# Block 1's doubled input in two transfers of 64 partitions from SP, and block 0's taps ahead of the first weights on DVE

## The chip, the core and the metric

The kernel runs on one core of one Trainium2 chip. The metric is the device time of one execution in microseconds. The core's engines are called PE (TensorE, matrix products), PEld (its weight load), DVE (VectorE), ACT (ScalarE), POOL (GpSimd) and SP (SyncE, which here only issues transfers). Each engine works through its own list of instructions in order.

## The reference: what is computed

```python
w = np.exp(weight - max); w = w / (sum(w) + 1e-9)      # 8 heads, 7 taps each
x_unf = x_pad[:, idx, :].reshape(B, S, K, H, group)    # causal windows of 7 tokens
x = np.einsum('hk,bskhg->bshg', w, x_unf)              # x becomes 8192 tokens x 192 channels
h = x @ w_in                                           # 192 -> 2048
g = np.where(h >= 1, h, np.where(h <= -1, 0, (h + 1) ** 2 / 4))
x = g @ w_out                                          # 2048 -> 192
h = x @ w_in2
x = (h * sigmoid(1.702 * h)) @ w_out2
```

A softmax-weighted convolution of seven taps along the tokens is followed by two feed-forward layers with different gates.

## The kernel before, in words

Data lie with the channels on the partitions. The 8192 tokens are 16 blocks of 512. The 192 channels are 128 ("a") and 64 ("b"); `xa[i]` holds the a part of block i with 6 tokens of lead, 128 rows of 518, and `xb` holds the b parts of two blocks in one tile.

Each number is split into a high and a low part (`fp32r`), and a product is made of three matmuls: high by high, low by high, high by low. A matmul takes half of the rows (64) of the array, and two of them run side by side on the two halves. Work on a block and a layer is a phase, (1, 0) being layer 1 of block 0. A phase has 16 units of 128 hidden channels. For two units at a time PE makes the first product into a `pair` tile, ACT and DVE make the gate and split it (`a`, then `ghi` on ACT and `glo` on DVE), and two such steps later PE adds the second product into `acc`. Step k stands for units 2k and 2k+1 of the whole list. The units of the first two phases, which are blocks 0 and 1 of layer 1, are mixed, so that each weight tile serves both while later weights are still being prepared.

The weights come as 64-bit floats. A weight tile (layer n, group g) lands in `raw`, and then ACT scales its high words (`wa`, L148), DVE shifts the low words (`wd`, L151) and joins both (L154), ACT or DVE casts the high part (L160), and DVE subtracts to get the low part (L165, L170). For the first two groups this is done in two pieces, the first of 448 columns. For later groups `convert_at` places these operations by step numbers: the table `steps` gives for each group the step of its fetch, scale, shift, join, high and low. Operations of one step on DVE run before that step's gate. `raw` has three buffers, so a fetch waits until an older tile has been scaled and shifted.

The convolution of the first two blocks is done in a special way, to be ready early:

- Block 0's a part (`ca`, operations `a0`): seven taps on DVE (L190, L191).
- The b part of both blocks (`cb_ps`, operations `b_ops`): PE, with the taps on diagonal matrices (`diag`, L237).
- Block 1's a part (`ca_ps`, operations `a1`): PE takes two taps in one matmul (L226). For that its input is doubled: tile `pair_x[j]` holds channels 64j to 64j+63 twice, on partitions 0 to 63 as they are and on partitions 64 to 127 shifted by one token. ACT first writes the seventh tap into the bank (`tap6`, L245), and the first of PE's three pairs of taps follows.

The program then runs lists of these operations in a written order, and `sc`, `sh`, `jo`, `hi`, `lo` are the five weight operations with the group number and an "o" for the second piece. `a0h`, `a0l`, `b0h`, ... are the splits of the convolution sums (`xah`, `xbh` on ACT at L250, `xal`, `xbl` on DVE at L253). PE's own order is: `b_ops`, the first piece of `a1`, the first products of units 0 and 1 (`straight`, `last`, `crossed`), the rest of `a1`, the first products of units 2 and 3, then the regular steps.

In the kernel before, ACT issues the two loads of `pair_x`, one for each tile of 128 partitions. The source is written with the shift as its outermost dimension, which has two entries:

```python
nc.scalar.dma_start(t, shifted(xa[1, j * H : (j + 1) * H], 0, 1, [PAD + T, H], [1, PAD + T]))
```

SP issues all other loads: `taps`, block 0's `xa`, the first `xb`, then the weights. The semaphores of transfers go round, eight of them, so an issue waits until the transfer eight places before has landed.

Of the kernel before, what the change touches and what calls it, by code (L numbers as in the profile page):

```python
# [8 lines left out]
F32 = mybir.dt.float32  # L9
# [6 lines left out]
P = 128  # L16
T = 512
# [3 lines left out]
def kernel(  # L21
# [21 lines left out]
    nc = tc.nc  # L43
    NBLK, D, _ = out.shape
    K = taps_in.shape[2]
    NF, _, WT = w1.shape
# [3 lines left out]
    PAD = K - 1  # L50
    H = P // 2
# [8 lines left out]
    xt_p = ctx.enter_context(tc.tile_pool(name="xt", bufs=2))  # L60
# [38 lines left out]
        nc.vector.reciprocal(share, share)  # L99
        nc.gpsimd.tensor_mul(taps, exps, share.unsqueeze(2).to_broadcast([P, 2, K]))  # L100

    def shifted(src, first, shift, *rest):
        return bass.AP(tensor=src.tensor, offset=src.offset + first, ap=[[shift, 2], *rest])

    def in_halves(t):
        return t.rearrange("(s p) c -> s p c", s=2)


    words = {1: w1, 2: w2}
# [396 lines left out]
    def finish(p, step):  # L506
        n, i = phases[p]
        if n == 1:
            up, down, add, bh, bl, ah, al = finish_ops(p)
            if i < B:  # L510
                groups = [(up, down, add, ah, al, bh, bl)]
            else:
                groups = [(up, ah, al), (down, add), (bh, bl)]
            for k, ops in enumerate(groups):
                for op in ops:
                    at(step + 2 * k, op) if k else op()
        else:
            acc_a, acc_b = accs.pop(p)
            o = o_p.tile([P, 2, T], F32, tag="o", name="o")
            nc.scalar.copy(o[0:DB, 1], acc_b[DB:P])  # L520

            def rest():
                nc.vector.tensor_add(o[0:DB, 1], acc_b[0:DB], o[0:DB, 1])
                nc.scalar.copy(o[:, 0], acc_a)
                nc.sync.dma_start(out[i, 0:P], o[:, 0])
                nc.sync.dma_start(out[i, P:D], o[0:DB, 1])

            if p < len(phases) - 1:
                at(step + 2, rest)
            else:  # L530
                nc.vector.tensor_add(o[0:DB, 1], acc_b[0:DB], o[0:DB, 1])
                near, far = slice(0, T // 2), slice(T // 2, T)
                nc.scalar.copy(o[:, 0, near], acc_a[:, near])
                nc.sync.dma_start(out[i, 0:P, near], o[:, 0, near])
                nc.scalar.copy(o[:, 0, far], acc_a[:, far])
                nc.scalar.dma_start(out[i, 0:P, far], o[:, 0, far])
                nc.sync.dma_start(out[i, P:D], o[0:DB, 1])
# [10 lines left out]
    plan, xt, raw = {}, {}, {}  # L548
# [26 lines left out]
    def fetch_x(*which):  # L575
        for part, i in which:
            xt[part, i] = x_load(part, i)
# [11 lines left out]
    with tc.manual_schedule():  # L589
        first, second = halves_of  # L590
        nc.sync.dma_start(taps, taps_in)
        fetch_x((0, 0), (1, 0))
        for g in (0, 1):
            fetch_w(1, g, first)
        for g in (0, 1):
            fetch_w(1, g, second)

        cb_ps, ca_ps = [bank(k, f"cb_ps{k}") for k in (3, 1)], bank(2, "ca_ps")
        warm_up(ca_ps, (T, T // 4), True)
        make_identity(nc, ident)  # L600
        less_max(taps)
        nc.scalar.activation(exps, taps, AF.Exp)

        es_ps = bank(0, "es_ps")[:, 0 : 2 * K].rearrange("p (j k) -> p j k", k=K)
        spread_exps(es_ps)
        warm_up(ca_ps, (7 * T // 8,), False)
        table = const.tile([P, 1], F32, name="table")
        for i in range(B):
            x1[i] = new_xs()
        ca = cv_p.tile([P, T], F32, tag="cva", name="cva")  # L610
        a0 = conv_taps(0, xt[0, 0], ca, exps)
        db = o_p.tile([P, K, P], F32, tag="o", name="diag")
        db = [db[:, k] for k in range(K)]
        diagonals(1, db[0:2])
        nc.scalar.copy(exps_s, es_ps)
        diagonals(1, db, 2)
        da = [f32(t).rearrange("p (k c) -> p k c", c=H) for t in new_xs()[0:2]]
        da = [[d[:, m] for m in range(K // 2)] for d in da]
        double_diagonals(da)
        wide = a_p.tile([P, 2, T], F32, tag="a", name="xt1").rearrange("p k t -> p (k t)")  # L620
        pair_x = [xt_p.tile([P, T + 128], F32, tag="xt0", name="xt"), wide]
        pair_x = [t[:, 0 : PAD + T] for t in pair_x]
        for j, t in enumerate(pair_x):
            nc.scalar.dma_start(t, shifted(xa[1, j * H : (j + 1) * H], 0, 1, [PAD + T, H], [1, PAD + T]))  # L624
        b_ops = conv_by_quarters(xt[1, 0], cb_ps, db)
        a1 = conv_by_sides(pair_x, ca_ps, da)
        tap6 = last_tap(pair_x, ca_ps)

        def run(*ops):
            for op in ops:  # L630
                op()

        def parts_of(g):
            s, made = raw.pop((1, g)), weight_tiles()
            return [weight_ops(1, g, s, lambda: made, cols) for cols in halves_of]

        def put_sum(i, part):
            c = (cb_ps[i] if part else ca if i == 0 else ca_ps)
            hi, lo = x1[i][2:] if part else x1[i][:2]
            return [lambda: high_of_sum(part, hi, c), lambda: low_of_sum(part, hi, lo, c)]  # L640

        steps = ((0, 1, 1, 1, 2, 2), (0, 2, 2, 3, 4, 5), (1, 3, 3, 4, 4, 6), (2, 5, 5, 6, 6, 7), (3, 7, 7, 8, 8, 9))
        steps += ((5, 8, 8, 9, 9, 10), (6, 10, 10, 11, 11, 12), (8, 11, 12, 13, 13, 14), (9, 12, 14, 15, 15, 16))
        steps += ((11, 15, 16, 16, 16, 17),)
        for k, when in enumerate(steps, 2):
            convert_at(1 + k // NG, k % NG, *when)
        for g in range(4, NG):
            k = 10 + 2 * g
            convert_at(2, g, k - 3, k - 1, k, k, k, k + 1)
        for j in range(1, NBLK // B):  # L650
            conv_at(j)

        def of(ops, step):
            return ops.get(step, [])

        (sc0, sh0, jo0, hi0, *lo0), (sc0o, sh0o, jo0o, hi0o, *lo0o) = parts_of(0)
        (sc1, sh1, jo1, hi1, *lo1), (sc1o, sh1o, jo1o, hi1o, *lo1o) = parts_of(1)
        (a0h, a0l), (b0h, b0l), (b1h, b1l), (a1h, a1l) = (put_sum(*k) for k in ((0, 0), (0, 1), (1, 1), (1, 0)))
        run(*b_ops)
        run(lambda: nc.scalar.activation(table, ident[:, 0:1], AF.Gelu_apprx_sigmoid))  # L660
        run(*a0[0:5], softmax_taps, sc0, sh0, jo0, hi0, *tap6, *a0[5:], sc1, *lo0, sh1, a0h, a0l, jo1, b0h, b0l)
        straight, crossed, last, closing = first_only(0)
        run(a1[0], straight, last, lambda: crossed(closing), *a1[1:])
        run(hi1, sc0o, sc1o, sh0o, jo0o, *lo1, hi0o, sh1o, b1h, jo1o, *lo0o, b1l)
        early, square, bound, high, low = gate_ops(0)
        run(early, lambda: square(0), lambda: square(1), lambda: bound(0), lambda: bound(1))
        run(*of(fetches, 0), a1h, a1l, lambda: high(0), lambda: high(1), lambda: low(0), lambda: low(1), hi1o, *lo1o)
        straight, crossed, last, closing = first_only(2)
        run(straight, last, lambda: crossed(closing))
        early, square, bound, high, low = gate_ops(2)  # L670
        scale, (shift, join) = of(act, 1), of(dve, 1)
        run(*of(fetches, 1), early, lambda: square(0), lambda: square(1), shift, *scale, lambda: bound(0))
        run(lambda: bound(1), join, *(lambda f=f, k=k: f(k) for f in (high, low) for k in (0, 1)))

        def beside(step):
            for op in plan.get(step, []):
                op()

        def finish_if_last(u, step):
            if 0 <= u < len(units) and units[u][1] == NF - 1 and units[u][0]:  # L680
                finish(units[u][0], step)

        beside(0)
        beside(1)
        for u in range(LAG, len(units) + LAG + 4, 2):
            v, step = u - LAG, u // 2
            if u < len(units):
                both(u, v)
                run(*of(fetches, step), *of(dve, step))
                if v + 1 == unit_at[0, NF - 1]:  # L690
                    gates_beside_finish(u, 0, of(act, step))
                else:
                    gates(u, of(act, step))
            elif v < len(units):
                gemm2(v)
                gemm2(v + 1)
            beside(step)
            finish_if_last(v + 1, u + 1)
# [55 lines left out]
```

## Time and profile before

| | |
|---|---|
| runs | 1141.98, 1142.46, 1144.1 us, median 1142.46 |
| profiled execution | 1141.74 us, span of its instructions 1139.9 us |
| PE | 98% of the span, granted clock 0.993 of full speed on average |
| DVE, ACT | 62% and 73% of the span |

The span runs from the first instruction to the last; 1.84 us lie around it. Busy shares are means over the whole span, so the start of the kernel, which the change touches, has to be read in its own window. Starts of instructions below are in microseconds from the start of the span.

### The profile page before, as it was taken

To read this page: it belongs to the slowest core of one execution; us is meant where nothing else is said; L and a number is where in the kernel's file an instruction comes from. 1 tells how busy PE (TensorE), PEld (TensorE's weight loads), DVE (VectorE), ACT (ScalarE), POOL (GpSimd) and SP (SyncE) were. 2 spreads that over 40 slices of the span, in tenths; PEclk is the share of its full clock that TensorE was granted. 3 is DMA by queue.
4 is the path that set the end of the run, shared out by engine and by line. 5 is a ranking of instruction groups with operands and counts; after the bars stand their busy time and mean duration, and the time that the engine had idled before them with its cause. 6 is when DMAs were issued, how large, how long until landed. Compare 5 with 4: busy or idle time off the path is not lost.

```text
span 1139.9 us, 23934 instructions
## 1 busy us (share of the span) xinstructions
PE 1120.0 (98%) x9790; PEld 1095.8 (96%) x9790; DVE 710.5 (62%) x1098; ACT 831.0 (73%) x1312; POOL 5.3 (0%) x14
## 2 busy tenths in 40 slices
PE   4999999999999999999999999999999999999998
PEld 1788999999999999999999999999999999999998
DVE  3998758684656746566564755647566475665533
ACT  3999768876768777686776767767687776867764
POOL 1000000000000000000000000000000000000000
PEclk7999999999999999999999999999999999999999
DMA  3433101000000001000010000100001000000000
GB/s 120 143 108 112 29 24 52 1 1 10 25 29 15 2 24 29 11 15 10 16 29 11 15 10 15 39 3 14 11 15 38 15 1 10 16 10 15 1 1 28
DMA packets 23872, 30.71 MB, mean 27 GB/s; under 512 B 3284, under 2 KB 15828, under 8 KB 23764
## 3 DMA queue, kind: packets, MB, share of 16 engines
q1 hardware_dynamic: 23360, 28.53, 8.7%
q8 instruction: 77, 1.26, 0.5%
q10 hardware_dynamic: 404, 0.66, 0.2%
q14 instruction: 31, 0.25, 0.1%
HBM read 19.22 MB, written 6.29 MB: 22 GB/s over the span
## 4 chain that ended last, share of the span: by engine, by line
PE 97%; DMA 2%; SPq 0%; DVE 0%; ACT 0%; issue 0%; ACTq 0%; DVEq 0%
PE acc L449 50%; PE pair L449 46%; DMA xt<-in_xa_dram 1%; PE acc L423 0%; PE ca_ps L226 0%; SPq L128 0%; DMA raw<-in_w_dram 0%; ACT ghi L359 0%; ACTq L624 0%; DVE wd L154 0%; SPq L183 0%; DVE wt L165 0%; DVE glo L363 0%; ACT ca_ps L245 0%; DVE a L355 0%
## 5 line engine op out<-in xcount | busy, mean ns | idle before, releaser
L449 PE MATMUL acc<-ghi,wt 64*128 64x512 f32 x3048 | 678.0, 387 | 0.0
L449 PE MATMUL acc<-glo,wt 64*128 64x512 f32 x2032 | 586.4, 386 | 0.0
L449 PEld LDWEIGHTS acc<-ghi,wt 64*128 64x128 f32 x3048 | 488.8, 184 | 3.2
L363 DVE TENSOR_TENSOR glo<-a,ghi 128x512 fp32r<-128x512 f32 x512 | 342.7, 691 | 224.5 <-ACT ghi L359 206.3
L449 PE MATMUL pair<-xah,wt 64*128 64x512 f32 x2048 | 451.6, 388 | 1.2 <-DVE wt L165 1.1
L359 ACT CAST ghi<-a 128x512 fp32r<-128x512 f32 x512 | 314.8, 622 | 44.1 <-DVE a L355 34.9
L449 PEld LDWEIGHTS acc<-glo,wt 64*128 64x128 f32 x2032 | 338.1, 184 | 2.4
L449 PEld LDWEIGHTS pair<-xah,wt 64*128 64x128 f32 x2048 | 302.9, 185 | 7.6 <-ACT xbh L250 1.6
L449 PE MATMUL pair<-xal,wt 64*128 64x512 f32 x1024 | 306.8, 387 | 0.0
L449 PE MATMUL pair<-xbh,wt 64*128 64x512 f32 x1024 | 282.6, 386 | 0.0
L355 DVE SCALAR_TENSOR_TENSOR a<-pair,a 128x512 f32<-128x512 f32 x256 | 164.9, 686 | 164.5 <-PE acc L449 123.1
L348 ACT ACTIVATE a<-pair 128x512 f32<-128x512 f32 x256 | 152.4, 595 | 146.7 <-PE pair L449 146.7
L449 PE MATMUL pair<-xbl,wt 64*128 64x512 f32 x512 | 197.1, 387 | 0.0
L449 PEld LDWEIGHTS pair<-xbh,wt 64*128 64x128 f32 x1024 | 188.3, 185 | 1.3
L346 ACT ACTIVATE a<-pair 128x1024 f32<-128x1024 f32 x128 | 131.6, 1028 | 66.3 <-PE pair L449 64.7
L449 PEld LDWEIGHTS pair<-xal,wt 64*128 64x128 f32 x1024 | 151.9, 185 | 1.3
L351 ACT ACTIVATE a<-a 128x512 f32<-128x512 f32 (+1 forms) x242 | 146.4, 649 | 4.1
L449 PEld LDWEIGHTS pair<-xbl,wt 64*128 64x128 f32 x512 | 94.1, 184 | 0.6
L191 DVE SCALAR_TENSOR_TENSOR cva<-xt,taps,cva 128x512 f32<-128x512 f32 x84 | 63.0, 750 | 1.5
L191 DVE SCALAR_TENSOR_TENSOR cvb<-xt,taps,cvb 128x512 f32<-128x512 f32 x42 | 31.5, 750 | 0.7
L154 DVE SCALAR_TENSOR_TENSOR wd<-wa,wd 128x768 uint32<-128x768 uint32 (+2 forms) x18 | 15.6, 867 | 4.0 <-ACT wa L148 3.4
L226 PE MATMUL ca_ps<-xt,xah 128*64 128x512 f32 x6 | 3.9, 761 | 14.0 <-ACT ca_ps L245 14.0
(68 smaller groups left out, 255.9 us busy)
## 6 DMA issues: line engine op xcount, KB each, us to landing
raw<-in_w_dram SPq DMA_DIRECT2D x48, 128.0 KB, 2.2
xt<-in_xa_dram SPq DMA_DIRECT2D x15, 259.0 KB, 2.8
out_dram<-o SPq DMA_DIRECT2D x15, 256.0 KB, 2.0
raw<-in_w_dram SPq DMA_DIRECT2D x48, 64.0 KB, 2.3
raw<-in_w_dram SPq DMA_DIRECT2D x16, 192.0 KB, 2.6
out_dram<-o SPq DMA_DIRECT2D x17, 128.0 KB, 2.2
xt<-in_xb_dram SPq DMA_DIRECT2D x8, 259.0 KB, 3.1
xbh<-xbh SPq DMA_DIRECT2D x14, 128.0 KB, 2.2
```

Source lines behind the costliest of these rows:

```text
L154: nc.vector.scalar_tensor_tensor(d(), a().bitcast(U32), 3, d(), op0=ALU.logical_shift_left, op1=ALU.bitwise_or)
L191: return lambda: nc.vector.scalar_tensor_tensor(c, x, w, c, op0=ALU.mult, op1=ALU.add)
L226: nc.tensor.matmul(c[side], d[j][m], x, start=False, stop=m == K // 2 - 1)
L346: nc.scalar.activation(a[:, k], h[:, k], AF.Relu, bias=0.5, scale=0.5)
L348: nc.scalar.activation(a[:, k], h[:, k], AF.Gelu_apprx_sigmoid)
L351: nc.scalar.activation(a[:, k], a[:, k], AF.Square)
L355: nc.vector.scalar_tensor_tensor(a[:, k], h[:, k], 1.0, a[:, k], op0=ALU.max, op1=ALU.min)
L359: nc.scalar.copy(halves[u + k][0], a[:, k])
L363: nc.vector.tensor_sub(lo, a[:, k], f32(hi))
L449: mm = nc.tensor.matmul(banks[n], w, r, start=n in fresh, stop=ends.get(n) == k)
```

## The change

SP issues the input of `pair_x`, ahead of the weights, in two transfers. Each goes to 64 partitions and fills both slots (j = 0 and 1), with the rows as the outermost dimension on both sides. ACT issues none of them. The doubled tile moves into the buffer `o` (each of its two rows 32 elements longer), and the diagonals move into a buffer of `a`. The order on ACT and DVE at the start changes, and so do two rows of `steps`.

```diff
-    def shifted(src, first, shift, *rest):
-        return bass.AP(tensor=src.tensor, offset=src.offset + first, ap=[[shift, 2], *rest])
+    def load_twice(t, src):
+
+        _, rows, width = src.shape
+        for s in (0, 1):
+            moved = bass.AP(tensor=src.tensor, offset=src.offset + s, ap=[[width, rows], [rows * width, 2], [1, width]])
+            nc.sync.dma_start(t[s * H : (s + 1) * H], moved)
...
-            o = o_p.tile([P, 2, T], F32, tag="o", name="o")
+            o = o_p.tile([P, 2, T + 32], F32, tag="o", name="o")[:, :, 0:T]
...
         fetch_x((0, 0), (1, 0))
+        pair_x = o_p.tile([P, 2, T + 32], F32, tag="o", name="xt")[:, :, 0 : PAD + T]
+        load_twice(pair_x, xa[1].rearrange("(j p) c -> j p c", j=2))
+        pair_x = [pair_x[:, j] for j in (0, 1)]
...
-        db = o_p.tile([P, K, P], F32, tag="o", name="diag")
-        db = [db[:, k] for k in range(K)]
+        db = a_p.tile([P, 2, T], F32, tag="a", name="diag").rearrange("p k t -> p (k t)")
+        db = [db[:, k * P : (k + 1) * P] for k in range(K)]
...
-        wide = a_p.tile([P, 2, T], F32, tag="a", name="xt1").rearrange("p k t -> p (k t)")
-        pair_x = [xt_p.tile([P, T + 128], F32, tag="xt0", name="xt"), wide]
-        pair_x = [t[:, 0 : PAD + T] for t in pair_x]
-        for j, t in enumerate(pair_x):
-            nc.scalar.dma_start(t, shifted(xa[1, j * H : (j + 1) * H], 0, 1, [PAD + T, H], [1, PAD + T]))
...
-        steps = ((0, 1, 1, 1, 2, 2), (0, 2, 2, 3, 4, 5), (1, 3, 3, 4, 4, 6), (2, 5, 5, 6, 6, 7), (3, 7, 7, 8, 8, 9))
+        steps = ((0, 1, 1, 1, 2, 2), (0, 2, 3, 3, 3, 4), (1, 4, 4, 5, 5, 6), (2, 5, 5, 6, 6, 7), (3, 7, 7, 8, 8, 9))
...
-        run(*a0[0:5], softmax_taps, sc0, sh0, jo0, hi0, *tap6, *a0[5:], sc1, *lo0, sh1, a0h, a0l, jo1, b0h, b0l)
+        run(*a0[0:5], softmax_taps, *tap6, *a0[5:], sc0, sh0, a0h, jo0, hi0, a0l, b0h, *lo0, sc1, sh1, b0l)
...
-        run(hi1, sc0o, sc1o, sh0o, jo0o, *lo1, hi0o, sh1o, b1h, jo1o, *lo0o, b1l)
+        run(sc0o, jo1, hi1, sh0o, jo0o, sc1o, *lo1, hi0o, sh1o, b1h, jo1o, *lo0o, b1l)
```

On ACT, at the start, after the diagonals, the rows of before are these (`wa<-raw 128x448` is `sc0` or `sc1`, `ca_ps<-xt` is `tap6`):

```order
L624 DMA xt<-in_xa_dram 128x1x518
L624 DMA xt_166<-in_xa_dram 128x1x518
L660 ACT_TABLE_LOAD
L660 ACTIVATE table<-ident 128x1
L148 ACTIVATE wa<-raw 128x448
L160 CAST wt_92<-wd 128x448
L245 ACTIVATE ca_ps<-xt,exps_s 64x512
L245 ACTIVATE ca_ps<-xt_166,exps_s 64x512
L148 ACTIVATE wa<-raw 128x448
L250 ACTIVATE xah<-cva,share 128x512
```

And of the change, at the same place:

```order
L659 ACT_TABLE_LOAD
L659 ACTIVATE table<-ident 128x1
L246 ACTIVATE ca_ps<-xt,exps_s 64x512 x2
L149 ACTIVATE wa<-raw 128x448
L251 ACTIVATE xah<-cva,share 128x512
L161 CAST wt_92<-wd 128x448
L251 ACTIVATE xbh<-cb_ps_120,share 128x512
L149 ACTIVATE wa<-raw 128x448
```

The two issues are gone, and `tap6` stands ahead of the first scaling instead of behind the first cast.

On DVE, after the reciprocal of the softmax (`wd<-raw` is `sh`, `wd<-wa,wd` is `jo`, `cva<-xt,exps,cva x2` the last two of block 0's seven taps), the rows of before are these:

```order
L151 TENSOR_SCALAR wd<-raw 128x448
L154 SCALAR_TENSOR_TENSOR wd<-wa,wd 128x448
L191 SCALAR_TENSOR_TENSOR cva<-xt,exps,cva 128x512 x2
L165 TENSOR_TENSOR wt_92<-wd,wt_92 128x384
L151 TENSOR_SCALAR wd<-raw 128x448
L253 SCALAR_TENSOR_TENSOR xal<-cva,share,xah 128x512
```

And of the change:

```order
L192 SCALAR_TENSOR_TENSOR cva<-xt,exps,cva 128x512 x2
L152 TENSOR_SCALAR wd<-raw 128x448
L155 SCALAR_TENSOR_TENSOR wd<-wa,wd 128x448
L254 SCALAR_TENSOR_TENSOR xal<-cva,share,xah 128x512
L166 TENSOR_TENSOR wt_92<-wd,wt_92 128x384
L152 TENSOR_SCALAR wd<-raw 128x448
```

The two taps come first, and the low part of block 0's sum comes ahead of the low part of the first weights.

On DVE in steps 2 to 5, the rows of before, from the low part of group 2 to the low part of group 3, are these (`a<-pair,a` and `glo` belong to the gates):

```order
L165 TENSOR_TENSOR wt_92<-wd,wt_92 128x640
L170 TENSOR_TENSOR wt_92<-wd,wt_92 128x2x64
L151 TENSOR_SCALAR wd<-raw 128x768
L355 SCALAR_TENSOR_TENSOR a<-pair_351,a 128x512 x2
L363 TENSOR_TENSOR glo<-a,ghi 128x512 x2
L154 SCALAR_TENSOR_TENSOR wd<-wa,wd 128x768
L151 TENSOR_SCALAR wd<-raw 128x768
L355 SCALAR_TENSOR_TENSOR a<-pair_420,a 128x512 x2
L363 TENSOR_TENSOR glo<-a,ghi 128x512 x2
...
L363 TENSOR_TENSOR glo<-a,ghi 128x512 x2
L165 TENSOR_TENSOR wt_92<-wd,wt_92 128x640
```

And of the change, over the same stretch:

```order
L166 TENSOR_TENSOR wt_92<-wd,wt_92 128x640
L171 TENSOR_TENSOR wt_92<-wd,wt_92 128x2x64
L356 SCALAR_TENSOR_TENSOR a<-pair_350,a 128x512 x2
L364 TENSOR_TENSOR glo<-a,ghi 128x512 x2
L152 TENSOR_SCALAR wd<-raw 128x768
L155 SCALAR_TENSOR_TENSOR wd<-wa,wd 128x768
L356 SCALAR_TENSOR_TENSOR a<-pair_418,a 128x512 x2
L364 TENSOR_TENSOR glo<-a,ghi 128x512 x2
L166 TENSOR_TENSOR wt_92<-wd,wt_92 128x640
```

The shift of group 3 has moved out of step 2 into step 3, and the low part of group 3 stands one gate earlier, in step 4. Group 4's shift, join and cast follow it a step later than before.

## Rows read from the trace of the kernel before

**Rows 1.** The page, part 1: busy time, share of span, instructions

```profile
PE 1120.0 (98%) x9790; PEld 1095.8 (96%) x9790; DVE 710.5 (62%) x1098; ACT 831.0 (73%) x1312; POOL 5.3 (0%) x14
```

**Rows 2.** Waits by engine, first 45 us: total us, times, longest us

```profile
PE ca_ps L226 <- ACT ca_ps L245: 14.0, 1, 14.0
...
ACT ca_ps L245 <- DMA xt<-in_xa_dram: 11.0, 2, 5.7
```

**Rows 3.** Chain that ended last, first 60 us: start, duration, what

```profile
9.29 15.46 DMA xt<-in_xa_dram
...
25.62 2.06 PE ca_ps L226 x4
27.69 2.25 PE pair L449 x10
29.98 0.96 PE pair L449 x6
30.94 1.87 PE ca_ps L226 x8
32.81 1.60 PE pair L449 x12
```

**Rows 4.** Windows: busy us of each engine, granted clock, DMA share, GB/s

```profile
2.00:8.00 6.00, 5.99 (x37) 2.43 (x40) 4.23 (x10) 2.54 (x10) 3.77 (x6) 1.00 0.76 226
...
6.00:8.00 2.00, 2.00 (x24) 0.64 (x20) 1.90 (x5) 0.00 (x0) 2.00 (x4) 1.00 0.68 186
...
18.00:24.00 6.00, 0.00 (x0) 0.00 (x0) 0.00 (x0) 0.69 (x1) 0.00 (x0) 0.50 0.13 50
...
26.00:28.00 2.00, 2.00 (x6) 0.39 (x5) 1.31 (x3) 1.23 (x3) 0.00 (x0) 0.50 0.00 0
...
60.00:80.00 20.00, 20.00 (x178) 16.55 (x178) 18.99 (x32) 18.57 (x24) 0.00 (x0) 1.00 0.35 100
```

**Rows 5.** Transfers issued in the first 8 us, the plain load: count, KB each, median us to landing

```profile
xt<-in_xa_dram SPq DMA_DIRECT2D x1, 259.0 KB, 2.6
```

**Rows 6.** ACT in order of time: start, duration, instruction, idle before and releaser

```profile
3.94 1.57 ACT L211 ACTIVATE diag<-ident,exps 128x128 f32<-128x128 f32 x5
...
9.85 1.28 ACT L660 ACT_TABLE_LOAD   x1 [4.33 <-DMA xt<-in_xa_dram]
11.14 0.20 ACT L660 ACTIVATE table<-ident 128x1 f32<-128x1 f32 x1
...
12.54 0.56 ACT L160 CAST wt<-wd 128x448 fp32r<-128x448 f32 x1 [0.69 <-DVE wd L154]
18.76 0.69 ACT L245 ACTIVATE ca_ps<-xt,exps_s 64x512 f32<-64x512 f32 x1 [5.66 <-DMA xt<-in_xa_dram]
```

**Rows 7.** DVE: timeline, its busy time in one window, one group of lines

```profile
7.90 0.17 DVE L99 RECIPROCAL share<-share 128x2 f32<-128x2 f32 x1
...
12.42 1.53 DVE L191 SCALAR_TENSOR_TENSOR cva<-xt,exps,cva 128x512 f32<-128x512 f32 x2
...
32.70 1.29 DVE L355 SCALAR_TENSOR_TENSOR a<-pair,a 128x512 f32<-128x512 f32 x2 [0.70 <-ACT a L351]
...
8.09:32.65 24.56, 8.28 (x17) 0.72 0.32 98
...
L154 DVE SCALAR_TENSOR_TENSOR wd<-wa,wd 128x448 uint32<-128x448 uint32 x2 | 1.2, 622 | 3.4 <-ACT wa L148 3.4
```

**Rows 8.** PE in order of time: the last of b_ops, and step 6

```profile
9.73 1.90 PE L237 MATMUL cb_ps<-xt,diag 64*64 64x512 f32 x16
...
54.25 0.50 PE L449 MATMUL pair<-xah,wt 64*128 64x512 f32 x2 [1.08 <-DVE wt L165]
```

**Rows 9.** DVE in steps 2 and 5, and PE where step 4 begins

```profile
42.11 0.56 DVE L151 TENSOR_SCALAR wd<-raw 128x768 uint32<-128x768 uint32 x1
...
44.01 1.29 DVE L363 TENSOR_TENSOR glo<-a,ghi 128x512 fp32r<-128x512 f32 x2
...
44.01 0.73 PE L449 MATMUL pair<-xah,wt 64*128 64x512 f32 x4
```

More of the change, by code (lines that the diff above doesn't have):

```diff
@@ L100, in softmax_taps @@
         nc.gpsimd.tensor_mul(taps, exps, share.unsqueeze(2).to_broadcast([P, 2, K]))
-    def shifted(src, first, shift, *rest):
-        return bass.AP(tensor=src.tensor, offset=src.offset + first, ap=[[shift, 2], *rest])
-    def in_halves(t):
-        return t.rearrange("(s p) c -> s p c", s=2)
+    def load_twice(t, src):
[3 more added lines that the diff above has]
+            nc.sync.dma_start(t[s * H : (s + 1) * H], moved)
     words = {1: w1, 2: w2}
```

## The prediction

> **What bounds the kernel now.** I read the busy shares first: PE is at work for 98% of the span [rows 1], so only time in which PE waits or runs slowly can be won. The waits name the place. Within the first 45 us PE waits once, for 14.0 us, for ACT to write `ca_ps`, and ACT in turn waits 11.0 us, in two pieces, for the two loads of `xt` that it issued itself [rows 2]. The chain of work that ended last goes the same way: 15.46 us of a transfer from 9.29 on, then ACT, then PE's `a1` at 25.62 [rows 3]. PE's part before it, `b_ops`, ended at 9.73 + 1.90 = 11.63 [rows 8].
>
> Two costs follow from that gap. The first is the gap itself. The second is the clock, which the windows show: it stands at 1.00 up to 8 us, at 0.50 (the 1.2 GHz level) in 18 to 24, where PE does nothing, and still at 0.50 in 26 to 28, where PE is busy again [rows 4]. In the chain, four matmuls of `a1` took 2.06 us there, while eight took 1.87 us later; the first products of units 0 and 1 (18 matmuls in two pieces, 27.69 to 30.94) took 3.25 us, while twelve such took 1.60 us at the full clock [rows 3], so 18 take 2.4.
>
> Later PE loses 1.08 us once, in step 6, to the low part of group 3's weights [rows 8]. From 60 us on PE is busy without a break [rows 4], and there nothing can be won.
>
> **The loads.** From 18 to 24 us almost nothing but the doubled loads moves, and the core moves 50 GB/s at a DMA share of 0.13 [rows 4]: 0.13 of 16 engines is two engines, at 25 GB/s each. The ordinary `xa` load, of the same 259 KB, landed in 2.6 us [rows 5].
>
> The rule of the Trainium skill that bears on this is in DMA: Bandwidth & Descriptors, section "Why a DMA increments its semaphore by 16 and not by 1": a transfer uses the largest number of engines up to 16 that divides the slowest dimension of both its sides. By it the old loads (128 and 2) get two engines, with which the trace's 0.13 agrees, and the new ones (64 and 64) get 16. The same page, section "Rules for kernel authors", speaks against halves: two transfers to disjoint halves of the partitions follow one another on the same engines, and one of 128 is advised. By that the two loads would simply come one after the other, as the bytes below are added up.
>
> No row shows a 64 x 2 x 518 transfer. The nearest rows are the plain `xa` load, as the good end, and 50 GB/s on two engines, as the bad end. I take the good end, since both sides now begin with rows as the plain load does.
>
> SP issues both loads ahead of the weights, so all weights queue behind 518 KB more. I add up bytes in SP's order: taps 7, four input loads of 259, the first pieces of groups 0 and 1 (448 each, by the shapes in the program) and their second pieces (320 each). At the mean rate of 2 to 8 us, 226 GB/s [rows 4], counted from 2 us, the doubled input has landed by 6.7 us, the first pieces by 8.8 and 10.8, the second by 12.2 and 13.7. The 186 GB/s of 6 to 8 us [rows 4] would make that 7.7, 10.2, 12.7, 14.4 and 16.2.
>
> **ACT and DVE at the start.** ACT's diagonals end at 5.51. Its table load of 1.28 us stood at 9.85 because of the two issues and their wait, with an activation of 0.20 behind it [rows 6]; now both follow at once, and ACT is free at 7.0. `tap6` is twice 0.69 [rows 6], to 8.4; the landing at 6.7 hides behind the table load. The first scaling runs to 9.0 if the weights are there (8.8 by the sum).
>
> DVE's reciprocal ends at 8.07, and the last two taps take 1.53 [rows 7], so they end at 9.6; shift and join end at 10.65 (join 0.62 [rows 7]). ACT's cast of 0.56 [rows 6] ends at 11.25, while DVE makes `xal`; then the low part, by 11.9. PE does not wait for that: `a1` runs at the full clock from 11.63, for half of 1.87 us, and the products of unit 0 begin at 12.55 instead of 27.69.
>
> What comes next is a chain of ACT and DVE up to unit 0's gate, which DVE began at 32.70 [rows 7]. Between 8.09 and 32.65 DVE was busy for 8.28 us [rows 7], and the change leaves all of these operations in place. Laid end to end from 8.07 they end at 16.35. They can't all follow closely, since sums and weights go to and fro between ACT and DVE; before, ACT's cast waited 0.69 us for such a hand-over [rows 6]. I allow two of these, 1.2 us, and put the gate at 17.55. **The chain is thus 15.15 us earlier.**
>
> PE by itself could be earlier still: 15.1 for the start (27.69 to 12.55) and 0.85 for the clock (3.25 to 2.4) make 16.0. So after the change the chain of ACT and DVE is the later one, and PE gets only what its slack allows. Moving group 3's shift out of step 2 takes 0.56 us [rows 9] off DVE ahead of that step's gate, hence 15.7 from there. In step 4 there is no slack: the gate's low parts end at 44.01 + 1.29 = 45.30, and PE needs the last of them at its seventh pair, about 6 x 0.23 us after 44.01 [rows 9], which is 45.4. I take **15.8 us** for PE up to step 5.
>
> **The step table.** Group 3's low part goes from step 5 to step 4, one step (19 pairs of matmuls, about 4.3 us at 0.23 a pair) earlier for its use in step 6, and the wait of 1.08 us [rows 8] goes. DVE's total up to step 5 is the same; group 4, first used in step 8, still has its low part in step 6. Added: **1.08 us**. If DVE's lag ate it all, nothing would be gained here; that is the lower bound.
>
> **Costed at nothing.** Longer rows of `o` leave the stores' rows as they are; the diagonals' buffer is free at 11.63, long before the second gate asks for it; ACT's two issues came in idle time. SP's two issues sit ahead of transfers whose landing is in the sum.
>
> **The sum.** 15.8 + 1.1 = 16.9 us. The profiled execution took 1141.74 us for a span of 1139.9; this gives a span of 1123.0 and an execution of 1124.8. The median of the runs lies 0.7 us above that execution, so I predict 1125.6 us, 1.5% faster.
>
> **The rivals.**
> - *The weights are late.* The doubled loads push them back, and the slower rate holds. For: 186 GB/s was measured with less in the queue. Against: those 2 us also had transfers waiting in SP's order. The second piece of group 1, wanted at about 14.25, would land at 16.2: 2.0 us on the chain, 1127.6.
> - *The wait in step 6 stays,* or one like it takes its place, since DVE was 95% busy from 60 to 80 us [rows 4] and now lags PE: 1126.7.
> - *The loads still go on two engines.* Then the change moves them without curing them. 518 KB at 50 GB/s last 10.6 us from 3.6 on, to 14.2; the weights' share behind them in the same two queues ends at 15.3; the first cast ends at 17.5 instead of 11.25, and the slow clock returns for `a1` and unit 0 (about 1 us beyond what the chain hides): 1133. Against: the shape.
> - *One engine, which is the slower side.* A load of 64 partitions with two slots might land on one engine and hold the weights behind it. At 25 GB/s the input lands at 24.8, as before, and the weights after it: the chain is some 1.7 us later than before, the table gives back 0.56 and 1.08, and the time is about 1142.5, no change. The deciding point is 22 GB/s, at which the landing is 2.3 us later and the kernel over 0.2% slower; at 20 GB/s it is 1147.5. Against: two engines were used by the old, worse shape.
>
> **How the numbers follow.** Forecast 72% (its own range 1123.5 to 1127.0), late weights 13%, wait stays 6%, two engines 5%, one engine 4% (half of it slower, half the same). The range 1123 to 1130 takes in the first three, with the runs' own spread of about 2 us. Above it lie the cases of few engines. 0.2% is about what a measurement of this kernel can tell from no change. Faster by more 0.96, within it 0.02, slower 0.02.
>
> **What would show it.** In the profile after: the two loads land within 7 to 8 us; ACT's table load stands at about 5.5; the first matmul of `pair` is near 12.6, and no idle time of PE over 1 us lies between 11.6 and 20; the granted clock is 1.00 throughout; unit 0's gate on DVE is near 17.5; no wait of PE for L166 about step 6. The prediction is wrong if the DMA share is low after 5 us with PE idle, if ACT waits for `raw` after 9 us, or if PE stalls on DVE in steps 2 to 8, which would mean that I took DVE's lag too lightly.

## The result, and the profile after

The changed kernel took 1125.92 us (median of four runs, 1125.27 to 1126.92), against 1142.63 us for the kernel before in the same measurement: a ratio of 0.9853, with a 95% interval of 0.9836 to 0.987. Its four spans were 1125.1, 1124.8, 1123.5 and 1123.5 us. The profiled execution was the slowest of the four, 1126.92 us with a span of 1125.1.

The page of that execution, parts 1 and 4 (busy time by engine; the chain that ended last, by engine and by line), is to be held against [rows 1]. Line numbers are one higher than before.

```profile
PE 1120.3 (100%) x9790; PEld 1068.8 (95%) x9790; DVE 709.9 (63%) x1098; ACT 830.4 (74%) x1312; POOL 5.6 (0%) x14
...
PE 100%; ACT 0%; issue 0%
```

PE now works for the whole span. The view of waits that showed 14.0 us in [rows 2] has no entry for PE between 3 and 60 us, nor is there one about step 6, where [rows 8] had 1.08 us. What PE does at the start, in order of time (start, duration, instruction):

```profile
5.59 8.43 PE L238 MATMUL cb_ps<-xt,diag 64*64 64x512 f32 x56
...
14.96 0.73 PE L450 MATMUL pair<-xah,wt 64*128 64x512 f32 x4
...
22.65 0.40 PE L450 MATMUL acc<-ghi,wt 64*128 64x512 f32 x2
```

The gap ahead of `a1` is closed, but `b_ops` end at 5.59 + 8.43 = 14.02, not at the 11.63 of [rows 8], and unit 0's products begin at 14.96. The 56 matmuls are the same as before. Why they take longer is seen in the weight loads between them (view of the engine's loads; in brackets the idle time ahead):

```profile
7.36 0.24 PEld L238 LDWEIGHTS cb_ps<-xt,diag 64*64 64x64 f32 x4 [0.61 <-issue]
8.21 0.24 PEld L238 LDWEIGHTS cb_ps<-xt,diag 64*64 64x64 f32 x4 [0.61 <-ACT ca_ps L246]
...
10.41 0.14 PEld L238 LDWEIGHTS cb_ps<-xt,diag 64*64 64x64 f32 x4 [0.29 <-issue]
10.85 0.14 PEld L238 LDWEIGHTS cb_ps<-xt,diag 64*64 64x64 f32 x4 [0.29 <-issue]
```

Up to 10 us a group of four comes every 0.85 us and takes 0.24; from 10.41 on one comes every 0.43 us and takes 0.14. PE ran at half pace for the first part of `b_ops` and at full pace after it, one to two as its levels of 1.2 and 2.4 GHz stand, though it was never idle in between. The windows (columns as in [rows 4]) show the same by the number of matmuls, while the column of the granted clock, ahead of the DMA share, stays at 1.00:

```profile
6.00:8.00 2.00, 2.00 (x12) 0.49 (x8) 1.86 (x6) 1.93 (x4) 2.00 (x4) 1.00 1.08 256
...
10.00:12.00 2.00, 2.00 (x24) 0.70 (x20) 2.00 (x4) 0.89 (x2) 0.00 (x0) 1.00 0.81 216
```

Twelve matmuls in 6 to 8 us, where [rows 4] had 24, twice as many; both rows give the clock as 1.00. In the first row that is no reading. The trace's own list of granted clocks has nothing before 10.05 us in this execution: its first entry is 1.00 from there on, and the column counts time without an entry as full. The pace of the groups changes at that moment. The durations agree with the lower level too: the matmuls of `b_ops` take 1.05 to 1.11 us each before 10 us and 0.59 later, and those of `a1`, also of 512 columns, take 1.06 to 1.11 where the list has 0.50 (ACT's loads, below) and 0.59 to 0.64 where it has 1.00. So the half pace is most likely the clock at its lower level.

The row of 6 to 8 us gives the DMA share as full and 256 GB/s, where the doubled loads alone had 0.13 and 50 GB/s before [rows 4]. The list of transfers issued from 2 to 16 us (count, KB each, median us to landing) has them as follows:

```profile
xt<-in_xa_dram SPq DMA_DIRECT2D x2, 259.0 KB, 4.5
```

ACT, in order of time, is to be held against [rows 6]:

```profile
5.56 1.28 ACT L659 ACT_TABLE_LOAD   x1
...
7.08 1.41 ACT L246 ACTIVATE ca_ps<-xt,exps_s 64x512 f32<-64x512 f32 x2
8.95 0.62 ACT L149 ACTIVATE wa<-raw 128x448 f32<-128x448 f32 x1 [0.46 <-DMA raw<-in_w_dram]
...
10.63 0.56 ACT L161 CAST wt<-wd 128x448 fp32r<-128x448 f32 x1 [0.31 <-DVE wd L155]
14.06 0.69 ACT L251 ACTIVATE xbh<-cb_ps,share 128x512 fp32r<-128x512 f32 x1 [2.86 <-PE cb_ps L238]
```

The table load stands at 5.56, `tap6` follows without a wait, so the doubled input was there by 7.08, and the first weights held ACT up for 0.46 us. All of this is as forecast. The last row is not: ACT waited 2.86 us for PE to finish `b_ops`. DVE, in order of time, waited behind it:

```profile
11.71 0.39 DVE L152 TENSOR_SCALAR wd<-raw 128x448 uint32<-128x448 uint32 x1
14.78 0.75 DVE L254 SCALAR_TENSOR_TENSOR xbl<-cb_ps,share,xbh 128x512 fp32r<-128x512 f32 x1 [2.69 <-ACT xbh L251]
...
19.60 1.29 DVE L356 SCALAR_TENSOR_TENSOR a<-pair,a 128x512 f32<-128x512 f32 x2 [0.20 <-ACT a L352]
```

The last row is unit 0's gate, forecast for 17.55. So after the change the two other engines wait for PE. The time came out within 0.4 us of the forecast, while this relation was forecast the other way round. The experiments ask whether the sum was right for its own reasons.

### The profile page after: what moved, and what is told of

It is laid out like the page before. It is cut to its first block, busy times and chain, and to the rows that moved or that the text cites. A ratio compares the mean times of both kernels' runs of the same rounds, so it can differ in the third digit from the quotient of the medians.

```text
span 1125.1 us, 23934 instructions
## 1 busy us (share of the span) xinstructions
PE 1120.3 (100%) x9790; PEld 1068.8 (95%) x9790; DVE 709.9 (63%) x1098; ACT 830.4 (74%) x1312; POOL 5.6 (0%) x14
## 3 DMA queue, kind: packets, MB, share of 16 engines
q8 instruction: 77, 1.26, 0.5%
## 4 chain that ended last, share of the span: by engine, by line
PE 100%; ACT 0%; issue 0%
PE acc L450 51%; PE pair L450 47%; PE cb_ps L238 1%; PE acc L424 0%; PE ca_ps L201 0%; PE ca_ps L227 0%; PE es_ps L208 0%; ACT o L534 0%; ACT o L536 0%
## 5 line engine op out<-in xcount | busy, mean ns | idle before, releaser
L450 PEld LDWEIGHTS pair<-xah,wt 64*128 64x128 f32 x2048 | 299.2, 184 | 10.8 <-PE pair L450 1.0
L79 ACT CAST xbh<-cvb 64x512 fp32r<-64x512 f32 x14 | 8.7, 619 | 10.1 <-DVE cvb L192 9.9
```

The lines of the kernel that those rows point to most:

```text
L79: nc.scalar.copy(hi, src)
L450: mm = nc.tensor.matmul(banks[n], w, r, start=n in fresh, stop=ends.get(n) == k)
```

## The experiments

One theory is that the time is set by PE's pace at the start: the moment at which PE comes to full pace varies, and the span follows the end of `b_ops`. A rival is that the new loads disturb PE while they run. Another is that the chain of ACT and DVE sets the time, as the prediction has it. Each kernel was measured beside the kernel before, whose median was 1142.76 us for the first repeat, the loads alone, the old table and the old order, 1142.79 for the old shape, ACT's loads, the table alone and the warm-up, and 1142.92 for the other three.

**The changed kernel again, unchanged,** twice.

> The changed kernel itself, once more, to see its executions beside one another. In the first profile of it PE made b_ops at half pace up to about 10 us (0.85 us for eight matmuls instead of 0.43) and ended them at 14.0 instead of 11.6 us. Theory A, the clock: the moment at which PE comes to its full pace is drawn anew in each execution. Then spans fall into groups between about 1123 and 1125.5 us, and this profile may show b_ops ending anywhere from 11.8 to 14.1 us. Theory B, contention: the two added loads or the new place of the diagonals slow the matmuls of b_ops down. Then this profile shows the half pace again, from 5.6 to about 10 us, and b_ops ends at 14.0, and all spans lie within 0.5 us of 1125.

> The changed kernel once more, beside the other two. Expected 1125.5 us within 0.5, and again another moment at which PE's matmuls in b_ops come to the full pace, anywhere from before 5.6 to about 10 us, with the span 1111.1 us above the end of b_ops.

(A group that comes every 0.85 or 0.43 us is four matmuls, not eight.) Measured: 1125.46 us (1124.69 to 1126.27), ratio 0.985 (0.9835 to 0.9865), and 1125.39 us (1124.72 to 1126.47), ratio 0.9851 (0.9838 to 0.9865). PE, ACT and DVE in the profiled execution of the second, in order of time:

```profile
5.40 6.24 PE L238 MATMUL cb_ps<-xt,diag 64*64 64x512 f32 x56
...
12.57 0.73 PE L450 MATMUL pair<-xah,wt 64*128 64x512 f32 x4
...
28.34 0.64 PE L450 MATMUL pair<-xah,wt 64*128 64x512 f32 x4
```

```profile
11.67 0.69 ACT L251 ACTIVATE xbh<-cb_ps,share 128x512 fp32r<-128x512 f32 x1 [0.59 <-PE cb_ps L238]
...
14.63 0.50 ACT L149 ACTIVATE wa<-raw 128x320 f32<-128x320 f32 x1 [0.35 <-DMA raw<-in_w_dram]
```

```profile
12.39 0.75 DVE L254 SCALAR_TENSOR_TENSOR xbl<-cb_ps,share,xbh 128x512 fp32r<-128x512 f32 x1 [0.42 <-ACT xbh L251]
...
17.67 1.29 DVE L356 SCALAR_TENSOR_TENSOR a<-pair,a 128x512 f32<-128x512 f32 x2 [0.66 <-ACT a L352]
```

And its window of 6 to 8 us:

```profile
6.00:8.00 2.00, 2.00 (x24) 0.64 (x20) 1.90 (x6) 1.93 (x4) 2.00 (x4) 1.00 1.03 274
```

Here PE had its full pace from the first of the 56 on: `b_ops` end at 11.64, unit 0 begins at 12.57, its gate at 17.67, and the span is 1122.9. The same program thus ends `b_ops` at 14.02, 12.70 or 11.64. The list of granted clocks begins at 10.05, 7.43 and 5.25 us in these three executions, always with an entry of 1.00, and the pace of `b_ops` rises there or, where the list begins before them, is full from the first. The same holds for every other run here. Over the profiled executions in which none of PE's work behind `b_ops` was altered, the span follows the end of `b_ops`:

| kernel | clock of 1.00 on record from, us | `b_ops` end, us | span, us | span less that end |
|---|---|---|---|---|
| changed kernel | 10.05 | 14.02 | 1125.1 | 1111.1 |
| three low parts (below) | 10.01 | 13.94 | 1125.0 | 1111.1 |
| short warm-up (below) | 8.91 | 13.08 | 1124.2 | 1111.1 |
| again, first | 7.43 | 12.70 | 1123.8 | 1111.1 |
| again, second | 5.25 | 11.64 | 1122.9 | 1111.3 |

In the last row 0.2 us is lost behind `b_ops`. In that execution ACT waited 0.35 us for a second piece of weights at 14.63, and unit 0's gate came 5.10 us behind unit 0's first products, where it is 4.64 in the first profile (19.60 less 14.96). That this is where the 0.2 us went is not shown. The loads were the same in both of the outer rows (256 and 274 GB/s in 6 to 8 us), at half and at full pace, so it is not the loads that slow PE.

**The loads alone:** the new transfers and buffers with both old lists and the old step table.

```diff
-        steps = ((0, 1, 1, 1, 2, 2), (0, 2, 3, 3, 3, 4), (1, 4, 4, 5, 5, 6), (2, 5, 5, 6, 6, 7), (3, 7, 7, 8, 8, 9))
+        steps = ((0, 1, 1, 1, 2, 2), (0, 2, 2, 3, 4, 5), (1, 3, 3, 4, 4, 6), (2, 5, 5, 6, 6, 7), (3, 7, 7, 8, 8, 9))
-        run(*a0[0:5], softmax_taps, *tap6, *a0[5:], sc0, sh0, a0h, jo0, hi0, a0l, b0h, *lo0, sc1, sh1, b0l)
+        run(*a0[0:5], softmax_taps, sc0, sh0, jo0, hi0, *tap6, *a0[5:], sc1, *lo0, sh1, a0h, a0l, jo1, b0h, b0l)
-        run(sc0o, jo1, hi1, sh0o, jo0o, sc1o, *lo1, hi0o, sh1o, b1h, jo1o, *lo0o, b1l)
+        run(hi1, sc0o, sc1o, sh0o, jo0o, *lo1, hi0o, sh1o, b1h, jo1o, *lo0o, b1l)
```

> The new loads and buffers with the old lists and the old step table. By the prediction's sum the loads carry nearly all: 15.8 of 16.9 us less what the order on ACT and DVE gives. In the old order tap6 stands behind the first scaling and cast, so it ends near 11.5 instead of 8.4 us, and block 0's two taps stand behind the first join; both are ahead of 11.6 us or close to it, so the order should give 0 to 1 us, and the wait of 1.08 us in step 6 stays unless PE is late anyway. Expected: 1126.5 to 1128 us. The rival, that the order on DVE matters as much as the loads, expects 1130 us or more.

Measured: 1128.26 us (1128.24 to 1128.54), ratio 0.9875 (0.986 to 0.989); 14.5 us of the gain are there, and the time is just above the range expected. The waits of PE from 3 to 60 us (total us, times, longest):

```profile
PE pair L450 <- DVE wt L166: 1.1, 1, 1.1
PE pair L450 <- DVE xbl L254: 0.2, 1, 0.2
```

The wait of step 6 is still there, and one for the low part of block 0's `b` sums is added. ACT, in order of time, shows what the old list does:

```profile
9.46 0.63 ACT L149 ACTIVATE wa<-raw 128x448 f32<-128x448 f32 x1 [2.35 <-DMA raw<-in_w_dram]
...
11.37 1.41 ACT L246 ACTIVATE ca_ps<-xt,exps_s 64x512 f32<-64x512 f32 x2
```

ACT stands idle for the weights for 2.35 us, with `tap6` behind them, whose input had long landed.

**The old step table in the changed kernel:** the first pair of lines of the diff above, alone.

> The changed kernel with the old step table. The prediction's term for the table is 1.08 us: group 3's low part is late in step 6, so a wait of PE of about 1 us stands there again and the time is 1 us above the changed kernel's, if the chain of ACT and DVE leads. The rival: PE is the later one now, as in the first profile of the changed kernel, DVE has slack, no wait comes back and the time is the changed kernel's within 0.3 us.

Measured: 1127.28 us (1127.05 to 1127.55), ratio 0.9866 (0.9851 to 0.9881). PE about step 6:

```profile
38.10 0.41 PE L450 MATMUL pair<-xah,wt 64*128 64x512 f32 x2
39.59 0.50 PE L450 MATMUL pair<-xah,wt 64*128 64x512 f32 x2 [1.08 <-DVE wt L166]
39.92 0.40 PE L450 MATMUL pair<-xal,wt 64*128 64x512 f32 x2
```

The same place in the first repeat of the changed kernel, in which `b_ops` ended within 0.05 us of this one:

```profile
37.91 0.62 PE L450 MATMUL pair<-xah,wt 64*128 64x512 f32 x4
38.36 0.39 PE L450 MATMUL pair<-xal,wt 64*128 64x512 f32 x2
```

The wait is the 1.08 us of [rows 8] to the hundredth, but the `xal` products come 39.92 − 38.36 = 1.56 us later. From start to start the waiting pair lies 1.49 us behind the one before it, instead of about 0.23, so the stall costs 1.26; the rest, 0.30, was lost just before it (0.19) and just behind it. The idle time that a row prints is counted from the modelled end of the matmul before it, and so it is less than what the stall costs. The spans differ by 1.5 us, the medians by 1.8.

**The new step table in the kernel before.** Its lists, loads and buffers stay.

```diff
-        steps = ((0, 1, 1, 1, 2, 2), (0, 2, 2, 3, 4, 5), (1, 3, 3, 4, 4, 6), (2, 5, 5, 6, 6, 7), (3, 7, 7, 8, 8, 9))
+        steps = ((0, 1, 1, 1, 2, 2), (0, 2, 3, 3, 3, 4), (1, 4, 4, 5, 5, 6), (2, 5, 5, 6, 6, 7), (3, 7, 7, 8, 8, 9))
```

> The kernel before with the new step table alone. In the kernel before PE waited 1.08 us in step 6 for group 3's low part; in the run with the old table on the changed kernel the gap between the two matmuls there was about 1.26 us above the usual one, and the kernel was 1.8 us slower by the medians. If this term stands by itself, the time is 1.2 to 1.8 us below the kernel before; if the wait only moves to another place, 0 to 0.4 us.

Measured: 1141.24 us (1140.28 to 1141.93), ratio 0.9986 (0.9977 to 0.9994): 1.55 us by the medians, anywhere from 0.7 to 2.6 by the interval. The traces narrow it: step 4 begins 0.66 us later than in [rows 9], at 44.67, and the pair that waited in [rows 8] comes 0.74 us earlier, at 53.51, so 1.4 us are won between them. Its PE row at the start says something else:

```profile
5.57 8.26 PE L237 MATMUL cb_ps<-xt,diag 64*64 64x512 f32 x56
```

Half pace to about 10 us here too, with the old loads, which ACT issues, and the old place of the diagonals. Neither causes it. In this kernel it costs nothing, since its `a1` begins only at 26.09; the closed gap is what brings it to light.

**The old order on ACT and DVE in the changed kernel:** the other four lines of the longer diff, alone.

> The changed kernel with the old lists on ACT and DVE at the start, and the new table. If the order matters, unit 0's products begin late because tap6 (ACT) waits for the first weights, their scaling and their cast: tap6 ends near 11.5 us, still ahead of b_ops' end at 11.6 to 14.0, so 0 to 0.5 us slower than the changed kernel. The rival, that block 0's taps ahead of the weights are what lets the gate come early, expects 1.5 us or more.

Measured: 1126.87 us (1126.44 to 1127.01), ratio 0.9862 (0.9845 to 0.9878), 1.4 us over the repeat by medians. Its `b_ops` ended at 13.47 and its span was 1125.0, which leaves 1111.5 behind them, 0.4 more than in the table. PE waits 0.24 us for `xbl`, and no more is seen. The order is worth something, between 0.4 and 1.4 us, which lies between the two things expected. The four runs lie within 0.6 us of one another, where those of the changed kernel lie within 1.6: with the old order an early full pace of PE seems to be lost again in that wait.

**The loads with the shift outermost again,** issued by SP at the new place.

```diff
-        for s in (0, 1):
-            moved = bass.AP(tensor=src.tensor, offset=src.offset + s, ap=[[width, rows], [rows * width, 2], [1, width]])
-            nc.sync.dma_start(t[s * H : (s + 1) * H], moved)
+        for j in (0, 1):
+            at_j = src.offset + j * rows * width
+            moved = bass.AP(tensor=src.tensor, offset=at_j, ap=[[1, 2], [width, rows], [1, width]])
+            nc.sync.dma_start(t[:, j], moved)
```

> The changed kernel, but SP's two loads in the old shape: one tile of 128 partitions each, the shift with its two entries outermost in the source. Place and order stay those of the change. The theory that the shape decides (two engines at 25 GB/s each) expects the core to move about 50 GB/s again at a DMA share near 0.13 for some 8 us, the doubled input to land at about 14 us, the weights behind it after 15 us, the first products of unit 0 at 19 to 20 us, and 1131 to 1134 us (the prediction's rival came to 1133). The rival theory, that the earlier place on SP is what helps, expects the changed kernel's 1125.5 us within 1 us.

Measured: 1133.74 us (1133.01 to 1134.43), ratio 0.9917 (0.9904 to 0.9931). Its windows, and ACT in order of time:

```profile
12.00:14.00 2.00, 0.00 (x0) 0.00 (x0) 0.00 (x0) 0.00 (x0) 0.00 (x0) 1.00 0.15 55
...
18.00:20.00 2.00, 1.66 (x8) 0.81 (x8) 2.00 (x5) 1.74 (x4) 0.00 (x0) 0.50 0.82 241
```

```profile
15.57 0.69 ACT L247 ACTIVATE ca_ps<-xt,exps_s 64x512 f32<-64x512 f32 x1 [4.47 <-DMA xt<-in_xa_dram]
16.85 0.61 ACT L150 ACTIVATE wa<-raw 128x448 f32<-128x448 f32 x1 [0.58 <-DMA raw<-in_w_dram]
```

This is the rival of two engines: 55 GB/s at a share of 0.15, the input there at 15.57, the weights behind it (9.4 us from issue to landing for those issued in the first 16 us), and the clock at 0.50 when PE comes back from its gap. It gives back 8 us of the 17. The rival said 1133.

**The new loads issued by ACT,** behind the diagonals; SP's order is then free for the weights.

```diff
-            nc.sync.dma_start(t[s * H : (s + 1) * H], moved)
+            nc.scalar.dma_start(t[s * H : (s + 1) * H], moved)
...
-        load_twice(pair_x, xa[1].rearrange("(j p) c -> j p c", j=2))
-        pair_x = [pair_x[:, j] for j in (0, 1)]
...
         double_diagonals(da)
+        load_twice(pair_x, xa[1].rearrange("(j p) c -> j p c", j=2))
+        pair_x = [pair_x[:, j] for j in (0, 1)]
```

> The changed kernel, but ACT issues the two loads in the new shape, behind the diagonals, so that SP's weights go first. The shape theory expects the two loads to land about 3 us after their issue, which can only come after ACT's diagonals (5.5 us) and the landing of an older transfer on the same semaphore (8.1 us before): issue 8 to 10 us, tap6 at 12 to 14 us and, since tap6 stands at the head of ACT's list, the first scaling after that: 1128 to 1130 us. The theory that the place alone decides expects more than 1138 us.

Measured: 1132.07 us (1131.4 to 1132.54), ratio 0.9904 (0.9889 to 0.9919), 2 us over the upper end of what was expected. ACT (ACTq is its sequencer) and PE in order of time:

```profile
8.69 2.55 ACTq L107 DMA_DIRECT2D xt<-in_xa_dram  x2
11.27 1.28 ACT L659 ACT_TABLE_LOAD   x1 [5.70 <-DMA raw<-in_w_dram]
...
14.42 1.41 ACT L246 ACTIVATE ca_ps<-xt,exps_s 64x512 f32<-64x512 f32 x2 [1.65 <-DMA xt<-in_xa_dram]
```

```profile
16.92 1.09 PE L227 MATMUL ca_ps<-xt,xah 128*64 128x512 f32 x1 [2.92 <-DMA xt<-in_xa_dram]
```

The issue itself came at 8.69 only. ACT waited for weights that SP had issued: the semaphores go round, so an issue waits for the transfer eight places before it, whoever issued that one. Behind the issue stood ACT's table load, 5.71 us later than in the changed kernel. The wait ahead of the issue had been expected (issue at 8 to 10 us). What had not is that the input took 5.9 us from issue to landing and not 3, so that `tap6` began at 14.42, and that the gap of PE, 2.92 us, brought the slow clock back: 0.50 from 16.80 to 20.22 us, with `a1` at 1.09 us a matmul instead of 0.64.

ACT's transfers have a queue of their own (q10), so this run also shows the new shape apart from SP's weights. In the window of 14 to 15 us (packets, MB, share of the 16 engines):

```profile
q10 hardware_dynamic: 81, 0.16, 74.6%
```

That is the work of about twelve engines and 160 GB/s, beside other transfers; in 18 to 24 us of the kernel before the same queue, with the old shape, had 10.9% and 0.25 MB in six times that span.

**The order's slack:** the low part of block 0's sum is made three times, 1.5 us more on DVE.

```diff
-        run(*a0[0:5], softmax_taps, *tap6, *a0[5:], sc0, sh0, a0h, jo0, hi0, a0l, b0h, *lo0, sc1, sh1, b0l)
+        run(*a0[0:5], softmax_taps, *tap6, *a0[5:], sc0, sh0, a0h, jo0, hi0, a0l, a0l, a0l, b0h, *lo0, sc1, sh1, b0l)
```

> The changed kernel with block 0's low part (a0l on DVE, 0.75 us) made three times instead of once, which puts 1.5 us of work into DVE's chain ahead of the low part of the first weights. If the chain of ACT and DVE were the later one at the start, as the prediction had it, the time would rise by about 1.2 to 1.5 us, to 1126.7 to 1127.2. If PE leads and DVE only waits for b_ops at that place (1.4 to 2.7 us of idle time ahead of xbl in the profiles so far), the time stays that of the changed kernel, 1125.5 us within 0.5.

Measured: 1125.97 us (1125.39 to 1126.81), ratio 0.9853 (0.984 to 0.9866), within the runs of the changed kernel. DVE in order of time:

```profile
10.44 2.32 DVE L254 SCALAR_TENSOR_TENSOR xal<-cva,share,xah 128x512 fp32r<-128x512 f32 x3
...
14.71 0.75 DVE L254 SCALAR_TENSOR_TENSOR xbl<-cb_ps,share,xbh 128x512 fp32r<-128x512 f32 x1 [1.18 <-ACT xbh L251]
```

The added work comes out of DVE's idle time, of which 1.18 us are left. In this execution, in which PE came to full pace at 10.01, the chain of ACT and DVE was not the one that set the time. A start at full pace with this added work was not profiled.

**How close that chain is:** `b_ops` do the first four of seven taps. This leaves out three taps of the `b` convolution of blocks 0 and 1, and shortens PE's part before unit 0.

```diff
-                    nc.tensor.matmul(c[o], d[k][r, r], t[r, k : k + T], start=k == 0, stop=k == K - 1)
+                    nc.tensor.matmul(c[o], d[k][r, r], t[r, k : k + T], start=k == 0, stop=k == 3)
...
-        return [lambda k=k: tap(k) for k in range(K)]
+        return [lambda k=k: tap(k) for k in range(4)]
```

> The changed kernel with only the first four of the seven taps in b_ops (the b part of blocks 0 and 1 then lacks three taps). That takes 3 of 7 parts off PE's 6.2 us of b_ops at the full pace, more where PE is still at half pace. If PE alone sets the end, the span stays the end of b_ops plus 1111.1 us, as in the three profiles of the changed kernel and of the shorter warm-up: b_ops ends near 9 to 11 us, and the time is 2.7 to 4 us lower, 1121.5 to 1122.8. If the chain of ACT and DVE is close behind PE, as it should be (gate of unit 0 not before 16.5 to 17.5 us against 18.3), most of it is not won: 1124 to 1124.8 us, and PE waits 1 to 2.5 us in front of unit 0's first products or shortly after.

Measured: 1124.52 us (1124.02 to 1124.6), ratio 0.9839 (0.9825 to 0.9852). PE in order of time:

```profile
5.15 3.67 PE L238 MATMUL cb_ps<-xt,diag 64*64 64x512 f32 x32
...
11.26 1.10 PE L450 MATMUL pair<-xah,wt 64*128 64x512 f32 x4 [1.43 <-ACT wt L161]
```

`b_ops` end at 8.82, 2.82 us earlier than in the second repeat, but the span, 1122.2, is only 0.7 us shorter. Now PE waits 1.43 us for the first cast, and unit 0's gate is at 16.95, 0.72 earlier than the 17.67 of that repeat. So even PE at its best could be only about 0.7 us earlier before that chain sets the time.

**A shorter second warm-up of PE,** 192 columns instead of 448, so that `b_ops` begin earlier.

```diff
-        warm_up(ca_ps, (7 * T // 8,), False)
+        warm_up(ca_ps, (3 * T // 8,), False)
```

> The changed kernel with the second warm-up on PE cut from 448 to 192 columns, which leaves the result as it is. The theory that PE alone now sets the end, from its first matmul on, expects b_ops to begin near 4.8 instead of 5.6 us, when its input has landed, and the time 0.7 to 0.9 us below the changed kernel's, 1124.7 us, unless the full pace of PE then comes later. The rival, that the chain of ACT and DVE is the later one (as the prediction had it), expects no change within 0.3 us.

Measured: 1125.64 us (1125.04 to 1126.23), ratio 0.9847; the 0.8 us expected are not seen. In the profile `b_ops` began at 4.85 instead of 5.59 and ended at 13.08, at half pace to about 8.9. At half pace an earlier start of 0.74 us is worth half of that, 0.37, less than the scatter of the runs. Inconclusive; no run here beats the changed kernel clearly with the whole computation done.

## Why the prediction was right, and where it was not

*The loads were right.* With the shift outermost they move 55 GB/s, with rows outermost they run with the others at a full share, and the input is there at 7.08 or before. The rival's 1133 us stood against 1133.74 measured, and its steps came in the order worked out (bytes, the weights queued behind, the slow clock), each 1.2 to 1.6 us late: the input was there at 15.57, the weights at 16.85 and the first cast at 18.71, against 14.2, 15.3 and 17.5. The rule of the Trainium skill on the slowest dimension of both sides (DMA: Bandwidth & Descriptors, section "Why a DMA increments its semaphore by 16 and not by 1") agrees with the runs: a share of 0.15 for 2 entries, and 0.75 for 64, by the queue of its own, with other transfers running beside it. That page's advice against two halves (section "Rules for kernel authors") does not reach this case, where cutting along the other axis costs 8 us.

*The weights are hardly late.* ACT waited 0.46 us for the first piece at 8.95; the sum by bytes had it land at 8.8. In the second repeat ACT also waited 0.35 us at 14.63 for the second piece of group 1, which the sum had at 13.7 and the rival at 16.2. That is one of the signs named for a wrong prediction (ACT waiting for `raw` after 9 us), but the rival's 2 us, 1127.6, did not come.

*The timetable was right when PE had its full pace.* In the second repeat `b_ops` ended at 11.64, unit 0 began at 12.57 and its gate at 17.67, for a span of 1122.9; forecast were 11.63, 12.55, 17.55 and 1123.0. Step 4 began at 28.34 instead of 44.01 [rows 9], 15.67 us earlier, where 15.7 to 15.8 were forecast.

*The step that failed* is "after the change the chain of ACT and DVE is the later one, and PE gets only what its slack allows". PE is the later one. In the first profile ACT and DVE waited 2.86 and 2.69 us for `b_ops`, and at full pace, in the second repeat, still 0.59 and 0.42. In a start at half pace 1.5 us more on DVE cost nothing, and with PE's part cut short the gate came at 16.95. That is 0.6 us over DVE's own work laid end to end (16.35), so the two hand-overs, for which I allowed 1.2 us, were too many by about one. That the figure of 17.55 came out is then partly chance: PE's 12.55 and the 4.64 us to the gate of the first profile make 17.19, and the rest, in that one execution, goes with ACT's wait for weights.

*Wrong too was "the granted clock is 1.00 throughout"* as a sign of full pace. The column says 1.00 where the trace has no entry, up to 10.05 us in that execution, and PE ran at half pace there. This puts the spans of one program anywhere from 1122.9 to 1125.1. I had taken the 11.63 of [rows 8] as a property of the kernel; it was one draw. The 1.00 read for 2 to 8 us in [rows 4] is of the same kind up to 5.16, where the list of the kernel before begins.

*The step table was mis-sized:* 1.08 us forecast, about 1.5 measured in the kernel before and 1.5 to 1.8 in the changed one, since the printed idle time is not the whole loss.

*The order on ACT and DVE had no term of its own;* it is worth 0.4 to 1.4 us. It is what lets `tap6` fill ACT's wait for the weights.

*The sum.* From the kernel before to the changed one with the old table, 1142.76 − 1127.28 = 15.5 us, against 15.8 forecast for loads and order. The table adds 1.8 by the same medians, 17.3 in all, against 16.9. The forecast of 1125.6 lies between the medians of 1125.39 and 1125.92. The errors are of the size of the scatter, which is why they don't show in the total.

*What stays open:* what decides the moment at which the granted clock comes to 1.00. It lies between 4.30 and 10.05 us in these runs, though PE is at work from 0.76 us on in all of them. That the kernel before scatters (1141.55 to 1144.19) for a like reason, behind its gap, is argued and not shown.

## What to carry to other kernels

Look at the outermost dimension of both sides of a transfer: two entries gave about 55 GB/s here and 64 gave a share of 0.75 beside other transfers, and a cure may be to cut the load along the other axis. Once a gap is closed, ask what it had hidden; here it hid PE's pace in the first 10 us, which now decides the spread of the runs. Read pace from the spacing of equal instructions, since a clock column may count time without an entry as full, and the cost of a stall from start to start.

## What the runs showed of the hardware that I had not expected

- TensorE, at work from 0.76 us on, ran its first matmuls at half pace until a moment that differs between executions of one program. The list of granted clocks begins there, with 1.00, at 5.25, 7.43 and 10.05 us (`b_ops` end at 11.64, 12.70, 14.02); for the time before, the column says 1.00 without an entry.
- A stall printed as 1.08 us of idle time cost 1.26 us from start to start.
- An issue on ACT waited for transfers of SP and held up a table load by 5.71 us.
- The runs of the two kernels that still have the wait in step 6 spread by 0.3 and 0.5 us, those of the changed kernel by 1.6 to 1.75. An early start of PE would be lost in that wait, which would explain it; this is argued. It can't be that wait alone, since the old order and the four taps, without it, spread by 0.6 us each; both have another wait of PE (0.24 and 1.43 us).
